# Opening of a Fourier filter and SoLU kernel: x transposed as interleaved pairs of columns and loaded in halves of 64 rows, raw weights loaded early, output weights converted in steps 0 and 1

## The chip, the cores and the metric

The kernel runs on one NeuronCore of a Trainium2 chip. A core has five engines that run their own instruction streams and meet at semaphores: TensorE (PE, whose weight loads the profile lists apart as PEld), VectorE (DVE), ScalarE (ACT), GpSimd (POOL) and SyncE (SP), and 16 DMA engines behind queues that SP, ACT and POOL fill. The metric is the device time of one execution in microseconds. Before the change it is 1617.99 us, the median of three runs (1617.08, 1617.99, 1620.11).

## The reference

The input x has 8 examples of 3136 rows and 256 columns. A global Fourier filter runs along the rows, and a feed-forward block with a SoLU and a layer norm follows, row by row.

```python
X = np.fft.rfft(x, axis=1)                                   # 8 x 3136 x 256
Y = X * (filt_r + 1j * filt_i)[None]
x = np.fft.irfft(Y, n=3136, axis=1).reshape(25088, 256)

h = x @ w_in                                                 # 256 -> 1024
e = np.exp(h - max(h)); solu = h * e / (sum(e) + 1e-9)
ln = (solu - mean(solu)) / sqrt(var(solu) + 1e-6) * g_ln
out = ln @ w_out                                             # 1024 -> 256
```

## The kernel before

A row number is split as 3136 = 49 x 64, and the transform is done as matrix products in two stages with 49-point and 64-point tables; in between, the data changes place between partitions. Rows n and N2-1-n of the 64 are treated together, as an upper half h = 0 and a lower half h = 1, which leaves NH = 32 places m for each of the 49 rows.

The work has two parts.

**The opening** (lines 415 to 631, first `ExitStack`) does example 0 on the chip, with nothing of it in DRAM. Its order is written out by hand (`tc.manual_schedule`), so every engine and every queue runs its instructions in the order of the code:

- SP, ACT and POOL issue the loads (526 to 555). `fetch_x` (509) brings x in eight pieces of four places for each half into `rows_x`, 128 partitions x 32 places x 256 columns; the first 48 of the 49 rows go by `fetch_x` and the last by `fetch_last_rows` (516). On SP then come the tables with the filters (`load_tables`, 462), three of four raw blocks of w_in (`begin`, 501), small tables, six pieces of example 1 (`fetch_second`, 457), and the filters go back to DRAM as `f_dram` (553). The weights are 64-bit floats that the kernel converts itself.
- The first products (`first_rows`, 557; PE line 558) multiply a piece of `rows_x` by `wf0_t`, and ACT copies the result back over `rows_x` (565, 572).
- `convert(0)` (585) turns raw block 0 into floats: nine DVE instructions (`load_float64`, 424, lines 430 to 444).
- `idle_row` (581) gives PE products that nobody reads; they multiply the first table by the first filter. `tables_back` (473) turns the tables through PE (480) and ACT (482).
- `turn_rows` (589, DVE line 591) transposes `rows_x` in place, 32 x 32 blocks, 64 columns in each of four instructions. It walks the 32 places for each column.
- A loop over seven units (611): `start(i + 2)` issues the forward products (PE line 318, into `pb`), `multiply` does the filter (DVE lines 339 and 340, POOL 341), `idle` keeps PE running, and `inverse` makes the back products (PE line 318, into `pc`), which ACT copies into `rows_x` (356). The third table turn stands in the loop at i = 2 (613).
- `turn_rows` again; then on DVE `convert` of blocks 2, 1 and 3 and `weight_sums` (162), four sums that a seven-product scheme for 2 x 2 blocks needs.
- `back` (402) makes the final products of example 0 (PE line 408) and ACT copies them into `y` (411).

**The steps** (1012 to 1151) work on blocks of 128 rows of `y`. Step k takes block k through the products with w_in (`product`, 759, PE line 767; `keep` and `finish` bring them out on ACT and DVE), exp, normalize, a DVE transpose (`turn`, 831), a regrouping by DMA, and, nine steps later (LAG), the products with w_out (`project`, 903). Beside that, the steps carry the Fourier work of examples 1 to 7, by the list `PLAN` (37): example 1's first products (`first`, 236, PE line 243, ACT copy 245, stored by POOL in `store_first`, 249) lie in steps 0 and 1, in each step four pieces early and four in the list `late`, its spectrum units from step 4 on. They use the two PSUM buffers of `ps_t`.

The output weights are prepared in the steps too: `load_w_out` (682) is issued before step 0, `convert_w_out(k)` (688) converts one quarter in each of steps 0 to 3 (nine DVE instructions and four of line 694 that scale by `g_sb`), and `prepare_w_out` (700) makes the mean over the rows with PE (712) and ACT (714), subtracts it (717) and makes four sums (162), in steps 3 and 4. In a step they stand ahead of the `late` jobs:

```python
        if k < 4:
            convert_w_out(k)
        if k == 3:
            prepare_w_out(0)
            prepare_w_out(1)
        if k == 4:
            for n in range(2, 7):
                prepare_w_out(n)
        for job in late[k] + loads[k]:
            job()
```

Of the kernel before, what the change touches and what calls it, by code (L numbers as in the profile page):

```python
# [17 lines left out]
P = 128  # L18
# [34 lines left out]
def dft_tables():  # L53
# [39 lines left out]
    wf0 = np.zeros((NR, 4, 32))  # L93
    wi0 = np.zeros((4, 32, NR))
    wf0[:, :, :NS] = wf.reshape(NR, NS, 4).transpose(0, 2, 1)
    wi0[:, :NS] = wi.reshape(NS, 4, NR).transpose(1, 0, 2)
    return wf.reshape(NR, NK).astype(f32), wf0.reshape(NR, P).astype(f32), wq.reshape(P, 2, 64).astype(f32), \
# [4 lines left out]
def kernel(  # L102
# [80 lines left out]
    def all_filter_rows(i0, n):  # L183

        for k, filt in enumerate((filt_r, filt_i)):
            for u in range(2):
                for quarter in range(2):
                    held = min(n, (NS - u + 1) // 2 - i0)
                    yield (slice(NQ * u + 32 * quarter, NQ * u + 32 * quarter + 32), k, held,
                           filter_rows(filt, quarter, u, i0, held))  # L190
# [10 lines left out]
    class Spectrum:  # L201
# [119 lines left out]
        def forward(self, i, pss):  # L321
            t2, de = self.t2s.pop(i), self.des[i]
            for u in range(self.shape(i)[0]):
                for r in range(2):
                    block = slice(NQ * r, NQ * r + NQ)
                    self.product(i, pss[r][NQ * u:NQ * u + NQ], lambda v: de[block, v, 0, u, :],
                                 t2[block, u::2, :])
# [18 lines left out]
        def inverse(self, i, pss, out=None):  # L346
# [6 lines left out]
            self.gs[i] = self.buffer(i, "g", [P, 4, C]) if out is None else out  # L353
            for u in range(self.shape(i)[0]):
                w = self.shape(i)[1]
                nc.scalar.copy(out=self.gs[i][:, u:2 * w:2, :], in_=pss[u][:, 0:w, :])
# [45 lines left out]
    def back(e, ch, cb, evac):  # L402
# [4 lines left out]
        for i in range(NCH):  # L407
            nc.tensor.matmul(out=psv[:, i:2 * NCH - i:2 * NCH - 1 - 2 * i, :],
                             lhsT=t4s[e, ch][:, i, cb * P:cb * P + P], rhs=wi_t, start=True, stop=True)
# [4 lines left out]

    with ExitStack() as st:
        fpool = pool("fp", 1, stack=st)
        pools = {name: pool(name + "0", bufs, stack=st)
                 for name, bufs in (("r", 1), ("p", 2))}
        rows_x = pools["r"].tile([P, NH, C], FP32, name="x_0", tag="r")
        pool("gap", 1, stack=st).tile([P, 5 * 4 * C], FP32, name="gap", tag="gap")  # L420
# [41 lines left out]
        def load_tables(i0, n, dma):  # L462
            de = fpool.tile([P, n, 2, 2, NQ], FP32, name=f"de_{i0}", tag=f"de{i0}")
            dma(out=de[:, :, 0].rearrange("p i u q -> p i (u q)"), in_=there_dram[:, i0:i0 + n, :])
            f = fpool.tile([P, n, 2, C], FP32, name=f"f_{i0}", tag=f"f{i0}")
            for place, k, held, rows in all_filter_rows(i0, n):
                dma(out=f[place, 0:held, k, :], in_=rows)
            for i in range(n):
                tables[i0 + i], filters[i0 + i] = (de, i), (f, i)
# [39 lines left out]
        def fetch_x(h, n0, n, r0, rows, dma):  # L509

            first, step = (n0, C) if h == 0 else (N2 - 1 - n0, -C)
            dma(out=rows_x[N1 * h + r0:N1 * h + r0 + rows, n0:n0 + n],
# [3 lines left out]
        def fetch_last_rows(h, odd, dma):  # L516

            row, first = N1 * h + N1 - 1, odd if h == 0 else N2 - NH + 1 - odd
            places = slice(odd, NH, 2) if h == 0 else slice(NH - 2 + odd, None, -2)
            dma(out=rows_x[row:row + 1, places],  # L520
                in_=bass.AP(tensor=x.tensor, offset=x[0].offset + ((N1 - 1) * N2 + first) * C,
                            ap=[[N2 * C, 1], [2 * C, NH // 2], [1, C]]))

        st.enter_context(tc.manual_schedule())
        wf0_t = fpool.tile([NR, P], FP32, name="wf0_t", tag="wf0")
# [3 lines left out]

        fetch_x(0, 0, NCH, 0, N1 - 1, nc.sync.dma_start)  # L530
        fetch_x(1, 0, NCH, 0, N1 - 1, nc.scalar.dma_start)
        for odd in range(2):
            for h in range(2):
                fetch_last_rows(h, odd, (nc.sync, nc.scalar)[h].dma_start)
        for i in range(1, pieces):
            fetch_x(0, NCH * i, NCH, 0, N1 - 1, nc.sync.dma_start)
            fetch_x(1, NCH * i, NCH, 0, N1 - 1, nc.gpsimd.dma_start)
            if i == 4:
                begin(0, nc.gpsimd.dma_start)
        load_tables(0, 4, nc.sync.dma_start)  # L540
        load_tables(4, 4, nc.sync.dma_start)
        load_tables(8, NP - 8, nc.sync.dma_start)
        for j in (2, 1, 3):
            begin(j, nc.sync.dma_start)
# [5 lines left out]
        fetch_second()  # L550
        for i0, n, rows in ((0, 4, P), (4, 4, P), (8, NP - 9, P), (NP - 1, 1, NQ)):
# [5 lines left out]
        def first_rows(ps, j, i, h):  # L557
            nc.tensor.matmul(out=ps[:, j], lhsT=wf0_t,
                             rhs=rows_x[0:NR, NCH * i:NCH * i + NCH, P * h:P * h + P], start=True, stop=True)

        for i in range(pieces - 2):
            ps = ps_h.tile([P, 2, 512], FP32, name=f"pa_0_{i}", tag="h")
            for h in range(KD):
                first_rows(ps, h, i, h)
            nc.scalar.copy(
                out=rows_x[:, NCH * i:NCH * i + NCH, :].rearrange("p m (h c) -> p h m c", h=KD),
                in_=ps.rearrange("p h (m c) -> p h m c", m=NCH))
        for h in range(KD):
            ps = ps_h.tile([P, 2, 512], FP32, name=f"pa_0_last_{h}", tag="h")
            for j in range(2):  # L570
                first_rows(ps, j, pieces - 2 + j, h)
            nc.scalar.copy(
                out=rows_x[:, NH - 2 * NCH:NH, P * h:P * h + P],
                in_=ps.rearrange("p j (m c) -> p (j m) c", m=NCH))
# [14 lines left out]
        def turn_rows(first, size=64):  # L589
            part = rows_x[:, :, first:first + size].rearrange("p m c -> p c m")  # L590
            nc.vector.transpose(out=part, in_=part)

        convert(0)
        idle_row(3, "idle")
        tables_back(0, 4)
        idle_row(3, "idles")
        tables_back(4, 4)
        for first in range(0, C, 64):
            turn_rows(first)
# [592 lines left out]
```

## Time and profile before

| what | value |
|---|---|
| median of three runs | 1617.99 us |
| the profiled execution: own time, span of its instructions | 1616.61 us, 1614.8 us |
| busy share of the span: PE, DVE, POOL, ACT | 96%, 79%, 70%, 57% |
| mean granted PE clock | 0.985 |
| first product on x, first forward product | 8.3 us, 41.1 us |
| second row of transposes, last back product of the opening | 68.4 us, 94.0 us |
| mean of the output weights on PE, first product with w_out | 140.7 us, 192.8 us |

The profile is of one execution. Times are from the start of its span. A row of a group has busy time and the mean of one instruction in ns, then the idle time of its engine just before, and who ended it. A row of the timeline has start, duration, engine, line, and in brackets the idle time before it and who ended it. [...] "PEclk" is the clock that was granted to PE, as a share of full speed.

### The profile page before, as it was taken

What the parts mean: (1) busy time and instruction counts of PE and PEld (TensorE: products, weight loads), DVE (VectorE), ACT (ScalarE), POOL (GpSimd) and SP (SyncE); (2) the same over time, 40 slices, a digit from 0 to 9 for tenths busy, and PEclk for the clock granted to TensorE, in tenths of its full rate; (3) what the DMA queues carried; (4) which work ended last, traced back from release to release, by engine and by line L of the source; (5) the groups of instructions that cost most, each with busy time, mean ns of one, the idle gap of its engine ahead of it and who ended that gap; (6) DMA issues with size and microseconds to landing.
All of it is one profiled execution on the core that took longest, in us unless ns stands there. A gap on an engine that the chain in (4) does not pass through costs nothing. (4 is left out here: it accounts for less than half of the span.)

```text
span 1614.8 us, 36632 instructions
## 1 busy us (share of the span) xinstructions
PE 1548.7 (96%) x12814; PEld 1063.0 (66%) x12814; DVE 1272.2 (79%) x2256; ACT 918.4 (57%) x1870; POOL 1136.9 (70%) x1335
## 2 busy tenths in 40 slices
PE   5895899999999999999999999999999999999997
PEld 2452466666666677666766676666676777777777
DVE  5787887898889879886899779886888777777673
ACT  2242565656555656566556656566556666666663
POOL 1441888669778877697678877788766766676765
PEclk9897999999999999999999999999999999999999
DMA  9534778786788678865787677866785454343434
GB/s 247 187 97 148 216 237 224 221 237 197 205 229 257 183 185 246 235 193 156 228 247 209 175 190 242 230 181 170 215 225 149 123 134 122 104 112 93 117 105 112
DMA packets 340920, 298.08 MB, mean 185 GB/s; under 512 B 28126, under 2 KB 310216, under 8 KB 340738
## 3 DMA queue, kind: packets, MB, share of 16 engines
q1 hardware_dynamic: 275362, 170.91, 40.0%
q0 software_dynamic: 30912, 91.49, 18.9%
q10 hardware_dynamic: 34464, 33.33, 6.9%
q8 instruction: 104, 1.70, 0.5%
q14 instruction: 78, 0.64, 0.1%
HBM read 118.02 MB, written 74.84 MB: 119 GB/s over the span
## 5 line engine op out<-in xcount | busy, mean ns | idle before, releaser
L903 PEld LDWEIGHTS o<-w_out_sb,solu_t 128*128 128x128 f32 x3136 | 381.7, 192 | 48.7 <-issue 43.5
L767 PE MATMUL m<-w_in_sb,s 128*128 128x512 f32 x784 | 399.3, 610 | 9.6 <-ACT h L777 4.2
L903 PE MATMUL o<-w_out_sb,solu_t 128*128 128x128 f32 x3136 | 401.2, 276 | 2.8 <-DVE ot L923 2.7
L903 PEld LDWEIGHTS o<-w_out_sb,u 128*128 128x128 f32 x2352 | 307.7, 192 | 138.4 <-issue 105.9
L767 PE MATMUL m<-w_in_sb,y 128*128 128x512 f32 x588 | 308.5, 608 | 9.3 <-DVE nmax L791 7.9
L903 PE MATMUL o<-w_out_sb,u 128*128 128x128 f32 x2352 | 310.9, 276 | 2.6 <-POOL u L746 2.1
L813 DVE SCALAR_TENSOR_TENSOR h<-e,h 128x1024 f32<-128x1024 f32 x196 | 296.2, 1511 | 0.0
L777 ACT COPY h<-m 128x512 f32<-128x512 f32 x294 | 173.3, 589 | 207.2 <-PE m L767 185.1
L919 ACT ACTIVATE ot<-o,rs_t 128x128 f32<-128x128 f32 x392 | 143.6, 368 | 246.8 <-PE o L903 244.4
L791 DVE CUSTOM_DVE_ANT_0 h<-m,h 128x512 f32<-128x512 f32 x196 | 134.2, 685 | 175.5 <-ACT h L777 101.7
L746 POOL TENSOR_TENSOR u<-solu_t 128x512 f32<-128x512 f32 x98 | 136.3, 1391 | 192.3 <-DMA solu_t<-turn 131.8
L821 ACT ACTIVATE h<-h,nmu 128x1024 f32<-128x1024 f32 x196 | 225.1, 1148 | 60.2 <-DVE turn L831 60.1
L831 DVE STREAM_TRANSPOSE turn<-h 128x1024 f32<-128x1024 f32 x196 | 243.1, 1240 | 3.5 <-DVE ot L923 0.3
L801 ACT ACTIVATE e<-h,nmax 128x1024 f32<-128x1024 f32 x196 | 225.4, 1150 | 7.7 <-DVE h L813 6.3
L746 POOL TENSOR_TENSOR u<-solu_t,u 128x512 f32<-128x512 f32 x98 | 135.8, 1385 | 96.7 <-PE o L903 95.0
L767 PEld LDWEIGHTS m<-w_in_sb,s 128*128 128x128 f32 x784 | 128.2, 191 | 96.3 <-issue 74.9
L923 DVE SCALAR_TENSOR_TENSOR ot<-o,rs_t,ot 128x128 f32<-128x128 f32 x299 | 103.7, 347 | 100.6 <-ACT ot L919 59.1
L746 POOL TENSOR_TENSOR u<-u,solu_t 128x512 f32<-128x512 f32 x98 | 159.7, 1630 | 15.2 <-PE o L903 8.5
L767 PEld LDWEIGHTS m<-w_in_sb,y 128*128 128x128 f32 x588 | 96.6, 191 | 104.1 <-issue 45.3
L746 POOL TENSOR_TENSOR solu_t<-solu_t,solu_t 128x512 f32<-128x512 f32 x98 | 150.9, 1540 | 0.9
L746 POOL TENSOR_TENSOR s<-y 128x128 f32<-128x128 f32 x196 | 99.9, 510 | 30.2 <-ACT y L411 29.7
L385 PEld LDWEIGHTS py<-wb_t,t 50*64 50x64 f32 x3584 | 57.8, 134 | 43.3 <-issue 19.4
(126 smaller groups left out, 1972.6 us busy)
## 6 DMA issues: line engine op xcount, KB each, us to landing
solu_t<-turn SPq DMA_DIRECT2D x780, 128.0 KB
out_dram<-ot SPq DMA_DIRECT2D x196, 128.0 KB
t<-d POOLq DMA_DIRECT2D x112, 200.0 KB, 6.8
d<-x POOLq DMA_DIRECT2D x100, 200.0 KB, 5.2
f<-f_dram POOLq DMA_DIRECT2D x39, 512.0 KB, 7.4
t<-d ACTq DMA_DIRECT2D x37, 512.0 KB
d<-g POOLq DMA_DIRECT2D x36, 512.0 KB, 5.0
x<-in_x_dram SPq DMA_DIRECT2D x112, 98.0 KB
```

The source lines that it names most:

```text
L385: nc.tensor.matmul(out=views[g][64 * h:64 * h + 64, cb, i, :], lhsT=t4[rows, i, c0:c0 + 64], rhs=wb_t[rows, 0:N1], start=True, stop=True)
L746: nc.gpsimd.tensor_tensor(out=out, in0=in0, in1=in1, op=op)
L767: nc.tensor.matmul(out=ms[j, bank], lhsT=lhsT, rhs=w_in_sb[:, w, :], start=m in (1, 2, 7), stop=True, skip_group_check=True)
L777: nc.scalar.copy(out=h_half(k, i), in_=ms[j, 0])
L791: nc.vector.tensor_tensor_reduce(out=h_half(k, i), in0=ms[j, bank], in1=h_half(*kept), scale=1.0, scalar=sofar, op0=ALU.add, op1=ALU.min, ...
L801: nc.scalar.activation(out=e, in_=hs[k], func=AFT.Exp, bias=nmaxs.pop(k)[:, 1:2], scale=-1.0, accum_out=esums[g][:, i:i + 1])
L813: nc.vector.scalar_tensor_tensor(out=solu, in0=e, scalar=SHRINK, in1=solu, op0=ALU.mult, op1=ALU.mult, accum_out=nmu)
L821: nc.scalar.activation(out=solu, in_=solu, func=AFT.Square, bias=nmu, scale=-float(DFF), accum_out=variances[g][:, i:i + 1])
L831: nc.vector.transpose(out=turns[g][:, :, i, :], in_=solus[k].rearrange("p (f j) -> p f j", j=32))
L903: nc.tensor.matmul(out=pos[p, bank], lhsT=lhs[:, f, :], rhs=w[:, f, :], start=f == 0 and (m in (1, 2, 7) or alone), stop=True, skip_group_ ...
L919: nc.scalar.activation(out=out_half(p, *to)[0], in_=pos[p, 0], func=AFT.Copy, scale=rs)
L923: nc.vector.scalar_tensor_tensor(out=ot, in0=pos[p, bank], scalar=rs, in1=out_half(p, *kept)[0], op0=ALU.mult, op1=ALU.add)
```

## The change

In the opening:

- x is loaded in 64 rows for each half instead of 49, the last row with the others; what lies beyond the 49 rows meets zeros in `wf0_t`, which now has 128 rows. Of the sixteen loads one is on ACT, eight on SP, seven on POOL.
- The raw blocks of w_in all go out on POOL, between the x pieces, in the order 0, 2, 1, 3. Blocks 0, 2 and 1 are converted before the first transposes, block 3 after the second.
- SP sends all tables and then all filters (`load_filters`, new), and the rows of the filters in another order, so that consecutive transfers go to partitions 0, 64, 32 and 96.
- Fourteen warm-up products stand ahead of the first products on PE. All three table turns stand before the forward products, with idle products between them.
- A first product covers two places and all 256 columns, and ACT writes its result as interleaved pairs: `pairs_x` is the same memory as `rows_x`, with the two columns of a pair of places next to each other. The transposes then walk 16 pairs for each column (`"p a c t -> p c a t"`). Forward products, back products and the copies of `inverse` take every second word.
- The product tiles of the opening have three buffers instead of two, and a placeholder tile of 20 KB a partition (`gap`) goes.
- The raw output weights have a buffer that exists from the start (`turn0`) and are loaded in the opening, behind `fetch_second` and ahead of the stores of the filters. That buffer later takes every second `turn` tile.

In the steps: two quarters of the output weights are converted in step 0 and two in step 1, and their scaling is on ACT. The mean is made in step 2, and the subtraction and sums are done in step 3.

The diff, cut to its core:

```diff
-    wf0 = np.zeros((NR, 4, 32))
+    wf0 = np.zeros((2, 64, 4, 32))
-    wf0[:, :, :NS] = wf.reshape(NR, NS, 4).transpose(0, 2, 1)
+    wf0[:, :N1, :, :NS] = wf.transpose(0, 1, 3, 2)
...
-            for u in range(2):
-                for quarter in range(2):
+            for quarter in range(2):
+                for u in range(2):
...
                     self.product(i, pss[r][NQ * u:NQ * u + NQ], lambda v: de[block, v, 0, u, :],
-                                 t2[block, u::2, :])
+                                 t2[block, u::2, :] if len(t2.shape) == 3 else t2[block, :, :, u])
...
             for u in range(self.shape(i)[0]):
-                w = self.shape(i)[1]
-                nc.scalar.copy(out=self.gs[i][:, u:2 * w:2, :], in_=pss[u][:, 0:w, :])
+                nc.scalar.copy(out=self.gs[i][:, u:2 * w:2, :] if out is None else out[:, 0:w, :, u],
+                               in_=pss[u][:, 0:w, :])
...
-                             lhsT=t4s[e, ch][:, i, cb * P:cb * P + P], rhs=wi_t, start=True, stop=True)
+                             lhsT=t4s[e, ch][:, i // 2, cb * P:cb * P + P, i % 2], rhs=wi_t,
+                             start=True, stop=True)
...
-                 for name, bufs in (("r", 1), ("p", 2))}
+                 for name, bufs in (("r", 1), ("p", 3))}
         rows_x = pools["r"].tile([P, NH, C], FP32, name="x_0", tag="r")
-        pool("gap", 1, stack=st).tile([P, 5 * 4 * C], FP32, name="gap", tag="gap")
+        pairs_x = rows_x.rearrange("p m c -> p (m c)").rearrange("p (a c t) -> p a c t", c=C, t=2)
...
+        for i in range(pieces):
+            fetch_x(0, NCH * i, NCH, 0, 64, nc.sync.dma_start)
+            fetch_x(1, NCH * i, NCH, 0, 64, nc.gpsimd.dma_start if i else nc.scalar.dma_start)
+            if i % 2:
+                begin((0, 2, 1, 3)[i // 2], nc.gpsimd.dma_start)
+        for load in (load_tables, load_filters):
+            for i0, n in ((0, 4), (4, 4), (8, NP - 8)):
+                load(i0, n, nc.sync.dma_start)
...
         fetch_second()
+        for n in range(4):
+            load_w_out(n, nc.sync.dma_start)
...
+        for j in range(14):
+            nc.tensor.matmul(out=ps_t.tile([P, P], FP32, name=f"warm_{j}", tag="t"), lhsT=one, rhs=one,
+                             start=True, stop=True)
+        for i in range(pieces):
             ps = ps_h.tile([P, 2, 512], FP32, name=f"pa_0_{i}", tag="h")
             for j in range(2):
+                nc.tensor.matmul(out=ps[:, j], lhsT=wf0_t,
+                                 rhs=rows_x[:, NCH * i + 2 * j:NCH * i + 2 * j + 2, :],
+                                 start=True, stop=True)
+            nc.scalar.copy(out=pairs_x[:, 2 * i:2 * i + 2].rearrange("p a c t -> p a t c"),
+                           in_=ps.rearrange("p a (t c) -> p a t c", t=2))
...
+        def turn_rows():
+            for first in range(0, C, 64):
+                part = pairs_x[:, :, first:first + 64].rearrange("p a c t -> p c a t")
+                nc.vector.transpose(out=part, in_=part)
+
+        for j in (0, 2, 1):
+            convert(j)
         idle_row(3, "idle")
-        tables_back(0, 4)
-        idle_row(3, "idles")
-        tables_back(4, 4)
-        for first in range(0, C, 64):
-            turn_rows(first)
+        for i0, n in ((0, 4), (4, 4), (8, NP - 8)):
+            tables_back(i0, n)
+            idle_row(2, f"idle_{i0}")
+        turn_rows()
...
         for i in range(units):
-            if i == 2:
-                tables_back(8, NP - 8)
...
-        for j in (2, 1, 3):
-            convert(j)
+        turn_rows()
+        convert(3)
         weight_sums(w_in_sb)
...
         for f in range(KF // 2):
             fg = KF // 2 * h + f
-            nc.vector.tensor_scalar(out=w_out_sb[:, i, f], in0=w_out_sb[:, i, f],
-                                    scalar1=g_sb[:, fg:fg + 1], scalar2=-1.0 / SHRINK,
-                                    op0=ALU.mult, op1=ALU.mult)
+            nc.scalar.activation(out=w_out_sb[:, i, f], in_=w_out_sb[:, i, f], func=AFT.Copy,
+                                 scale=g_sb[:, fg:fg + 1])
...
             nc.vector.memset(mean["ones"][:, 0:P], 1.0)
+            nc.vector.tensor_scalar(out=g_sb, in0=g_sb, scalar1=-1.0 / SHRINK, scalar2=None, op0=ALU.mult)
...
-            turns[g] = wk2.tile([P, DFF // 32, 4, 32], FP32, name=f"turn_{g}", tag="turn")
+            turns[g] = turn_pools[1 - g % 2].tile([P, DFF // 32, 4, 32], FP32, name=f"turn_{g}", tag="turn")
...
-        if k < 4:
-            convert_w_out(k)
-        if k == 3:
-            prepare_w_out(0)
-            prepare_w_out(1)
-        if k == 4:
+        if k == 0:
+            prepare_w_out(0)
+        if k < 2:
+            for n in range(2 * k, 2 * k + 2):
+                convert_w_out(n)
+        if k == 2:
+            prepare_w_out(1)
+        if k == 3:
             for n in range(2, 7):
                 prepare_w_out(n)
```

## The prediction

> **What bounds the kernel now.** I read the page first, then the PE's waits, then the opening instruction by instruction.
>
> ```profile
> span 1614.8 us, 36632 instructions
> ...
> PE 1548.7 (96%) x12814; PEld 1063.0 (66%) x12814; DVE 1272.2 (79%) x2256; ACT 918.4 (57%) x1870; POOL 1136.9 (70%) x1335
> ...
> PE   5895899999999999999999999999999999999997
> ```
>
> The PE is full from the sixth slice on (one slice is 40 us). Only the first 165 us have holes, so whatever the opening gains or loses reaches the end nearly one for one. The steps that follow never wait for a time of day. The timeline of the opening, with the idle time before an instruction in brackets:
>
> ```profile
> 24.60 16.38 DVE L591 STREAM_TRANSPOSE x<-x 128x2048 f32<-128x2048 f32 x4 [7.17 <-DMA f<-in_filt_r_dram]
> ...
> 41.12 4.75 PE L318 MATMUL pb<-x,de 64*64 64x256 f32 x48 [8.95 <-DVE x L591]
> ...
> 68.44 16.40 DVE L591 STREAM_TRANSPOSE x<-x 128x2048 f32<-128x2048 f32 x4 [4.49 <-ACT x L356]
> ...
> 76.76 17.25 PE L408 MATMUL py<-wi_t,x 128*128 128x98 f32 x128 [3.50 <-issue]
> ```
>
> Two rows of four transposes, 16.4 us each, stand on the path: x transform, row one, seven units of spectrum work, row two, back products (L408). The PE's waits after 100 us:
>
> ```profile
> PE m L767 <- DVE nmax L791: 9.0, 3, 3.9
> PE ps_mean L712 <- DVE ones L706: 7.8, 1, 7.8
> PE m L767 <- DVE w_in_sb L162: 3.2, 1, 3.2
> PE m L767 <- ACT h L777: 1.8, 2, 1.0
> ```
>
> All but the last are DVE late with weight conversions. So DVE sets the start of full speed, from 84.8 us (end of row two) to 158.1 us (end of the output weights).
>
> **The transposes.** The nearest rows:
>
> ```profile
> L591 DVE STREAM_TRANSPOSE x<-x 128x2048 f32<-128x2048 f32 x8 | 32.8, 4238 | 11.7 <-DMA f<-in_filt_r_dram 7.2 <-ACT x L356 4.5
> ...
> L831 DVE STREAM_TRANSPOSE turn<-h 128x1024 f32<-128x1024 f32 x196 | 243.1, 1240 | 3.5 <-DVE ot L923 0.3
> ```
>
> L591 jumps 1 KB at every element and takes 2.0 ns an element; L831 reads in order and writes runs of 32 and takes 1.2. The changed pattern jumps after every second element. Bounds for one transpose: 2.4 us (L831's rate) and 4.1 us (no gain). I take 2.4, because the cost should belong to a lone word: 0.43 us is the time of L430, which touches every second word of raw, and of L434 on adjacent words. A row becomes 9.6 us, 6.8 less.
>
> [...]
>
> **Loads.** Ahead of the first filters (f_0) stand now: x 16 x 256 KB = 4.19 MB (3.2 before), four raw weights 2.10 MB (one, 0.52, before), the tables 0.85 MB, f_0 itself 1.05 MB, small tables 0.13: 8.3 MB instead of about 5.2. From 4 to 14 us the queues moved 274 GB/s, POOL's 1.73 MB against SP's 0.92, and from 16 to 34 us, SP alone, 244. So POOL's weights go ahead of SP's filters. x and raw: 6.4 MB / 274 = 23.4 us from 2 us, x complete near 25; the remaining 1.9 MB at 244: 7.8 us. **f_0 lands near 33 us**, about 22 before by the same sum. Bounds: 31 to 36.
>
> [...]
>
> **The PE up to the forward products.** Fourteen warm-up products cover the wait for x; 16 products of 0.86 us then follow x as it lands, to about 26 us, and the last eviction (1.0 us, L565) ends at 27. Row one of DVE would end at 36.6, converts 0, 2 and 1 (4.65 us each, nine rows L430 to L444) hidden in the wait for x. But in the PE's queue, ahead of the forward products, stand three idle products that read f_0, then three table turns (13 products) with two idles after each. The idles take 0.90 us (12 records in 5.42 us), the turns 0.26: 9 x 0.90 + 13 x 0.26 = 11.5 us from 33 us. The PE has stood 7 us by then. Before, it stood from 32.2 and its granted clock fell to 0.50 by 36, and it was full again 4 us after 41.1; so 4 us at half speed add 2. Forward products start at 33.2 + 13.5 = **46.7**, against 41.1: the filters and not the transposes decide, and the faster row one is hidden.
>
> From first forward product to row two took 27.3 us. Off: the cold start (2.1 us to DVE's first multiply, now 1.2) and the table turn inside the loop (units are 2.95 us apart, one was 5.3): 3.2 less. The third product buffer saves DVE 4.1 us of waits for pc, but the cycle goes pc, ACT, idle, pc on the PE, so I take 0 (at most 2.4, if POOL's 2.55 us a unit decided). Row two starts at **70.8** (was 68.4) and ends at 80.4 (was 84.8). Back products need two of its transposes: 75.6, met by the six idles (70.0 + 5.4), so the PE comes warm; 16 x 0.90 us (0.49 copy + 0.41 wait each when warm) end at **90.0** (was 94.0).
>
> **Strided operands.** Forward products, L408's weights and ACT's copies touch every second word. No row shows this on PE or ACT. I take 0, as L430 against L434; the other end is the transposes' 2.0 / 1.2 = 1.65 times: L408 is bound by weight loads (PEld 17.1 us beside PE 17.2), so +9.3 us; forward products +2, copies +2. A gain is excluded: all these were contiguous.
>
> **Steps 0 to 5.** Converts 2 and 1 leave the tail: convert 3 and the sums (4.65 + 2.6) end at 87.6, was 103.1, so the 3.2 us wait at 102.5 goes. Two output quarters per step now, scaled by ACT: 4 x 0.37 us (L919, nearest) instead of 0.87 on DVE. This adds a wait. ACT is in order, and behind its scaling stand the evictions of the late x products (L243), which have two banks; so PE's third such product waits for the second conversion.
> - Step 0: 90.0 + 5.4 (products 1, 2, four early ones) + 1.8 = 97.2. DVE converts 92.8 to 102.2, ACT scales to 103.7, evicts to 104.3; two late products at half clock: 107.7 (109.5 before).
> - Step 1: + 6.1 = 113.8; DVE converts 114.7 to 124.0, ACT to 126.1, late products to 129.5 (119.2 before; here it is 10 late).
> - Step 2: four products and the mean (32 x 0.11): 136.9. The mean stood at 146.1.
> - Step 3: finishes, turn, normalize to 142.6, then subtract and sums 6.2: 148.8. Step 4's finish 149.6, its last products 150.5 (150.8 before).
> - Step 5: DVE owes 3.6 of step 4, then its finish: the product that started at 158.8 starts at 154.1.
>
> **Sum:** 4.7 us earlier. Against the profiled run (1616.6, span 1614.8) this is 1611.9; against the median 1618.0, which I predict for, **1613.3**. The raw output weights now load after x's second example, long before 92 us; the turn buffers keep their number.
>
> **Rivals.**
> 1. *The filters are not late* (0.20). The swapped order of the filter rows spreads consecutive transfers; were f_0 there when x is done (it needs 350 GB/s, seen at 34 to 38 us on the raw weights, 375), the transposes would decide: forward at 36.6, 10 us sooner, 1603. Against it: 244 to 274 in all of x and filters.
> 2. *Slower: strided weights in L408* (0.14). Each load costs up to 1.65 times; from 1.33 times (4.7 / 14.4) on all is lost; at 1.65 the time is 1622.6. For it: L591; against: L430.
> 3. *The transposes do not get faster* (0.08). Row one stays hidden (27 + 16.4 = 43.4 < 46.7). Row two: back products' second half at 70.8 + 16.4, ends 94.4, so 1617.7.
> 4. *Given back* (0.10): late stores of the x products (ten us late in step 1) hold up the spectrum loads of steps 4 to 8, or POOL, 98% full at 240 to 260 us, is the bound: 1616 to 1618.
>
> Forecast 0.48. Some 0.2% (3.2 us) is what a measurement can tell from no change. Faster: 0.40 of the forecast, rival 1 and a trace: 0.61. Same: rest of the forecast, rivals 3 and 4 mostly: 0.24. Slower: rival 2 and a little of rival 4: 0.15. The range reaches to rival 1's 1602 and part of the way to rival 2: 1602 to 1619.5.
>
> **What would show it.** Transposes of 2.2 to 2.5 us; a PE hole of some 7 us before the first idle, released by the filters, and forward products near 47; row two near 71; L408 at 0.11 us a weight load; L162 long before the products that need it; in steps 0 and 1 L243 waiting for ACT, and ACT for DVE, 5 and 10 us. Wrong, if the first idle doesn't wait, if L408's loads grow, or if DVE never leaves ACT waiting in step 1.

## The result, and the profile after

The changed kernel takes **1609.9 us** (median of five executions, 1607.3 to 1612.0) against 1618.0 in the same comparison (1617.1 to 1624.3): ratio 0.9939, 95% interval 0.9916 to 0.9961. Two more comparisons gave 0.9969 (0.9955 to 0.9982) and 0.9962 (0.9943 to 0.9981), with 12 executions of the changed kernel each: 5.4 and 5.8 us between the medians, where 4.7 were forecast. The first comparison's 8.1 us rests on five executions; the three intervals overlap. The profiled execution took 1609.97 us with a span of 1608.2 (before: 1616.61 and 1614.8).

The page of the changed kernel, its span, the busy times, and the PE's row of 40 slices:

```profile
span 1608.2 us, 36683 instructions
...
PE 1555.3 (97%) x12848; PEld 1066.7 (66%) x12848; DVE 1258.9 (78%) x2241; ACT 924.7 (58%) x1886; POOL 1141.3 (71%) x1338
...
PE   7976999999999999999999999999999999999997
```

DVE lost 13 us of work. The third slice (80 to 120 us) fell from 9 to 7: there is a new hole. The fourth is 6, where it was 5. First the timeline of the opening (start, duration, instruction, idle time before it and what ended that; x16 stands for sixteen equal records in a row, and PE has two records for each product, 32 for the sixteen of L568):

```profile
21.37 9.89 PE L568 MATMUL pa<-x,wf_t 128*128 128x512 f32 x16 [3.48 <-issue]
...
32.39 8.89 DVE L590 STREAM_TRANSPOSE x<-x 128x2048 f32<-128x2048 f32 x4 [3.30 <-ACT x L571]
34.02 4.41 PE L576 MATMUL idle<-f,de 128*128 128x512 f32 x6 [2.75 <-DMA f<-in_filt_r_dram]
...
46.41 3.06 PE L318 MATMUL pb<-x,de 64*64 64x256 f32 x48
...
70.80 8.89 DVE L590 STREAM_TRANSPOSE x<-x 128x2048 f32<-128x2048 f32 x4 [7.10 <-ACT x L357]
75.44 15.26 PE L410 MATMUL py<-wi_t,x 128*128 128x98 f32 x128
```

A row of four transposes takes 8.89 us instead of 16.4. But row one ends at 41.3 and the forward products start 5 us behind that: the idles of L576 waited for the filters (2.75 us, third row), and the table turns and idles behind them ran in order. The second half of the opening is the forecast to within 1 us. Next, steps 0 and 1, first by the PE's waits from 85 to 170 us, then ACT's scaling (L682) and the late products (L243) in the timeline:

```profile
PE pa L243 <- ACT y L245: 16.2, 2, 10.3
PE m L755 <- DVE nmax L779: 3.4, 1, 3.4
...
98.70 1.28 ACT L682 ACTIVATE w_out_sb<-w_out_sb,g_sb 128x128 f32<-128x128 f32 x4 [1.29 <-DVE w_out_sb L458]
103.42 1.27 ACT L682 ACTIVATE w_out_sb<-w_out_sb,g_sb 128x128 f32<-128x128 f32 x4 [3.44 <-DVE w_out_sb L458]
104.60 1.04 ACT L245 COPY y<-pa 100x512 f32<-100x512 f32 x2
...
105.21 3.73 PE L243 MATMUL pa<-y,wf_t 98*100 98x512 f32 x4 [5.84 <-ACT y L245]
...
127.12 3.73 PE L243 MATMUL pa<-x,wf_t 98*100 98x512 f32 x4 [10.34 <-ACT y L245]
```

Read the middle three rows from the end: ACT evicts the late products only at 104.60, because its queue holds the scaling of 103.42, which waited 3.44 us for DVE's conversion. The wait is PE's, the cause sits two engines away. The 16.2 us replace the 20 us of waits for DVE that the kernel before had.

### The profile page after: what moved, and what is told of

Its sections match the earlier page's. It is cut to its first block, busy times and chain, and to the rows that moved or that the text cites. A ratio compares the mean times of both kernels' runs of the same rounds, so it can differ in the third digit from the quotient of the medians.

```text
span 1608.2 us, 36683 instructions
## 1 busy us (share of the span) xinstructions
PE 1555.3 (97%) x12848; PEld 1066.7 (66%) x12848; DVE 1258.9 (78%) x2241; ACT 924.7 (58%) x1886; POOL 1141.3 (71%) x1338
## 5 line engine op out<-in xcount | busy, mean ns | idle before, releaser
L801 DVE SCALAR_TENSOR_TENSOR h<-e,h 128x1024 f32<-128x1024 f32 x196 | 307.8, 1570 | 0.0
L907 ACT ACTIVATE ot<-o,rs_t 128x128 f32<-128x128 f32 x392 | 143.2, 367 | 245.7 <-PE o L891 244.1
L819 DVE STREAM_TRANSPOSE turn<-h 128x1024 f32<-128x1024 f32 x196 | 243.1, 1240 | 3.1
L734 POOL TENSOR_TENSOR u<-solu_t,u 128x512 f32<-128x512 f32 x98 | 136.0, 1388 | 93.8 <-PE o L891 93.5
L755 PEld LDWEIGHTS m<-w_in_sb,s 128*128 128x128 f32 x784 | 129.0, 192 | 93.5 <-issue 73.1
L734 POOL TENSOR_TENSOR solu_t<-solu_t,solu_t 128x512 f32<-128x512 f32 x98 | 156.1, 1593 | 0.9
L734 POOL TENSOR_TENSOR s<-y 128x128 f32<-128x128 f32 x196 | 96.2, 491 | 26.5 <-ACT y L414 26.0
```

The lines of the kernel that those rows point to most:

```text
L734: nc.gpsimd.tensor_tensor(out=out, in0=in0, in1=in1, op=op)
L755: nc.tensor.matmul(out=ms[j, bank], lhsT=lhsT, rhs=w_in_sb[:, w, :], start=m in (1, 2, 7), stop=True, skip_group_check=True)
L801: nc.vector.scalar_tensor_tensor(out=solu, in0=e, scalar=SHRINK, in1=solu, op0=ALU.mult, op1=ALU.mult, accum_out=nmu)
L819: nc.vector.transpose(out=turns[g][:, :, i, :], in_=solus[k].rearrange("p (f j) -> p f j", j=32))
L907: nc.scalar.activation(out=out_half(p, *to)[0], in_=pos[p, 0], func=AFT.Copy, scale=rs)
```

## The experiments

The table has the profiles' marks in us: start of the forward products (L318), end of the back products (L410), end of the sums of the input weights (L162), start of the mean's product (ps_mean), then the 14th and the last turn transpose (L819, before L831); last the median time and the interval of the ratio to the kernel before. The medians come from five comparisons, in which the kernel before lay between 1617.3 and 1618.5.

| kernel | forward | back ends | sums | mean | turn 14 | last turn | median | ratio |
|---|---|---|---|---|---|---|---|---|
| before | 41.1 | 94.0 | 103.1 | 140.7 | 249.4 | 1583.6 | 1618.0 | 1 |
| before_again | 41.8 | 94.9 | 104.0 | 141.7 | 250.5 | 1582.5 | | |
| after | 46.4 | 90.7 | 86.9 | 135.5 | 246.2 | 1578.5 | 1609.9 | 0.9916 to 0.9961 |
| after_again | 45.1 | 89.4 | 85.6 | 135.3 | 247.2 | 1578.4 | | |
| after_third | 47.3 | 91.6 | 87.8 | 137.1 | 249.7 | 1585.9 | 1611.8 | 0.9955 to 0.9982 |
| after_fourth | 45.7 | 90.0 | 86.2 | 135.4 | 245.7 | 1578.8 | 1612.7 | 0.9943 to 0.9981 |
| early_idle | 39.5 | 83.8 | 80.0 | 129.0 | 240.3 | 1574.2 | 1605.8 | 0.9901 to 0.9939 |
| scale_last | 46.2 | 90.5 | 86.7 | 127.3 | 240.2 | 1570.5 | 1603.6 | 0.9896 to 0.9930 |
| both | 41.5 | 85.7 | 82.0 | 120.5 | 231.9 | 1568.9 | 1596.2 | 0.9855 to 0.9895 |
| quarters_late | 45.6 | 89.8 | 86.1 | 140.5 | 250.1 | 1584.3 | 1612.9 | 0.9964 to 0.9990 |
| no_pairs | 45.4 | 92.3 | 91.4 | 137.7 | 248.2 | 1579.9 | 1615.0 | 0.9968 to 0.9997 |
| raws_late | 40.5 | 84.7 | 93.8 | 137.2 | 248.5 | 1580.2 | 1612.4 | 0.9955 to 0.9980 |
| both_raws_late | 35.2 | 79.4 | 88.5 | 120.6 | 233.2 | 1564.3 | 1598.9 | 0.9858 to 0.9912 |
| both_spread | 39.4 | 83.7 | 79.9 | 128.2 | 236.6 | 1567.2 | 1601.7 | 0.9880 to 0.9935 |

The theory is the prediction's: two waits on the path, for the filters near 34 us and for ACT in steps 0 and 1, limit a gain that comes from DVE's relief. The rivals are that other parts carry the gain, or that something in the later steps does.

### What repeats: both kernels again

The first two profiles seemed to say that the opening's lead was lost at 246 us and a larger one appeared between 440 and 506 us. That could be the change or the single execution.

> The kernel before, unchanged, for a second profile. What is open: between the two first profiles the lead of the changed kernel was 3.3 us at the 14th turn (246 us), about 0 from the 15th to the 37th (263 to 440 us), and 7.3 us at the 45th (506 us). Theory A (chance of one execution: transfers that land a little sooner or later): the second profile does not pass the marks at the same times as the first; differences of 1 to 6 us against the first profile come and go at other turns. Theory B (the schedule is that rigid): it passes every turn within 0.5 us of the first profile, and the loss at 246 us and the gain at 440 to 506 us belong to the change.

> The changed kernel, unchanged, for a second profile. Theory A (chance of one execution): the lead over the kernel before at the 14th turn is again about 3 us, but the loss at 246 us or the gain between 440 and 506 us is not there, or is somewhere else. Theory B: 0.0 to +1.1 us at turns 15 to 37 and some -7 us from turn 45 on, again.

> The changed kernel unchanged, for more times and a third profile. The second profiles put the two kernels' spans 4.7 us apart (1612.9 and 1608.1), the medians of the first comparison 8.1. Theory A (what the opening saves, 3 to 4 us at the turns 15 to 29, is all; the rest of the 8.1 is the spread of single executions): the third profile passes turns 0 to 13 within 0.5 us of the second, and the median of the new executions lies 4 to 6 us under the kernel before's. Theory B (something in the later steps gains too): again 7 to 10 us between the medians, with the ends of the profiles 3 to 5 us further apart than turn 29.

> The changed kernel unchanged, as the measure for the two beside it on the same chip. If what the third comparison gave is right (1611.8 against 1617.25), the median is 1610 to 1613 again, 4 to 7 us under the kernel before's; if the first (8.1 us apart), 1608 to 1610.

Theory A of the first two holds. The loss at 246 us isn't in after_again (turns 15 to 21 are 3.0 to 3.7 us ahead of before_again), and of the gain from turn 37 to 45, 5.0 us are between the two profiles of the kernel before. After_third passed turn 14 2.5 us later than after_again and turn 45 10.7 us later (515.2 against 504.5): single executions drift apart by that much with nothing changed. On average over the four profiles of the changed kernel and the two of the one before, the lead is 2.7 us at turn 4 (166.7 against 169.4), 2.8 at turn 14 and 2.7 at the last turn: as far as six executions can say, what the opening gives reaches the end. In between it is not constant (-1.4 to 1.0 at turns 15 to 38, 2.0 to 5.0 from turn 45 on), by less than single executions drift. The medians, over more executions, say 5.4 and 5.8; after_fourth's 1612.7 fell in the first band of its expectation. Why the profiles show only half of that is not settled: the two profiled executions of the kernel before (1616.6 and 1614.7) are below its medians.

### The wait for the filters: early_idle

```diff
         def idle(out):
-            nc.tensor.matmul(out=out, lhsT=..., rhs=filters[0][0][:, 0], ...)
+            nc.tensor.matmul(out=..., lhsT=..., rhs=tables[0][0][:, 0:4, 0], ...)
```

> The idle products of the opening read a table that lands with x (de_0) in place of the filters f_0; their output goes nowhere, so nothing that is computed changes. Theory (the prediction's: the filters decide when the forward products start, because the idles ahead of them wait for f_0): the first idle starts right behind the x products, at 31 to 32 us instead of 34.0; the forward products then wait for row one of the transposes (ends 41.3) or for the idles, whichever is later: 41.5 to 43.5 us instead of 46.4; row two starts 3 to 5 us sooner (66 to 68 instead of 70.8), and if the opening's lead reaches the end, the time is 3 to 5 us less than the changed kernel's, 1605 to 1607. Rival 1 (the PE's cold clock takes it back: idles run at half speed): forward at 45 to 46, 1609. Rival 2 (the opening's lead is lost in steps 0 and 1, where ACT's block sets the pace from DVE's conversions): row two 3 to 5 us sooner but the turn of step 13 and the end as before, 1610.

The timeline of early_idle:

```profile
28.82 2.74 PE L576 MATMUL idle<-de 128*128 128x512 f32 x6
...
30.14 8.89 DVE L590 STREAM_TRANSPOSE x<-x 128x2048 f32<-128x2048 f32 x4 [1.39 <-DMA f<-in_filt_r_dram]
...
39.54 3.08 PE L318 MATMUL pb<-x,de 64*64 64x256 f32 x48
```

What a bracket names is inferred: row one reads no filter, and follows ACT's last eviction (ends 30.10). The six idle records take 2.74 us instead of 4.41 (the PE didn't stand before them), and the forward products start right behind the last idles, 0.5 us after row one (ends 39.0). The back products end 6.9 us sooner, 2 us more than expected. The expectation took row one's end from the changed kernel's first profile (41.3), where x was late; here row one started at 30.14 instead of 32.39, as in the other profiles of the changed kernel (30.2 to 30.7). The median is 6.0 us under the 1611.8 of after_third, which is from another comparison (the kernel before: 1617.7 here, 1617.3 there). Theory confirmed; both rivals fall.

### The wait for ACT: scale_last

```diff
         for job in late[k] + loads[k]:
             job()
+        if k < 2:
+            for n in range(2 * k, 2 * k + 2):
+                scale_w_out(n)
```

Here `scale_w_out` is the loop of four ACT instructions that `convert_w_out` ended with.

> In steps 0 and 1 the scaling of the output weights on ACT is issued behind the step's late evictions instead of ahead of them; all that is computed is the same. Theory (ACT, in order, holds the late x products): the PE's two waits for ACT's evictions (5.8 and 10.3 us) go; the late products of step 0 start near 99.5 instead of 105.2, those of step 1 near 117 instead of 127.1; then DVE with its four conversions (9.4 us a pair) sets the pace again, and the mean's product starts 5 to 9 us sooner (127 to 130 instead of 135.5), step 4's last product 3 to 8 us sooner (143 to 148 instead of 150.8); 1602 to 1607 if the lead reaches the end. Rival (DVE sets the pace anyway, and the waits only move to another place): the PE waits as long for DVE, step 4's last product at 150 to 151, 1610.

Its PE's waits from 85 to 170 us:

```profile
PE m L758 <- ACT h L768: 10.7, 4, 7.5
PE m L758 <- DVE nmax L782: 3.4, 1, 3.4
PE pa L243 <- ACT y L245: 2.2, 1, 2.2
```

The 16.2 us fall to 2.2, but 10.7 (2.3 before) are now for ACT's h (L768), which in turn stands behind the second scaling:

```profile
121.95 1.28 ACT L685 ACTIVATE w_out_sb<-w_out_sb,g_sb 128x128 f32<-128x128 f32 x4 [3.96 <-DVE w_out_sb L458]
```

Still the mean's product starts 8.2 us sooner, the 14th turn 6 us and the last 8 us; the median is 8.2 us under 1611.8. Theory confirmed, though 8.4 of the 14.0 us come back as another wait, as the rival has it. The rest is not all waiting. Between the last back product and the mean's product, the PE's idle time falls from 16.3 to 9.7 us and its busy time from 28.5 to 27.1, for the same work: in the changed kernel its granted clock there is 0.77, and the time of the products grows behind the waits. Of its late products, the four records behind the wait of 5.84 us took 3.73 us (granted clock 0.51 from 105.2 to 109.0 us), and four such records at 111.4 us took 1.94 (1.00 from 109 to 117); here the four behind the wait of 2.24 us took 2.77.

### Both edits

> The two edits together: the idles of the opening read a table that lands with x, and the scaling on ACT is issued behind the late evictions. Alone they ended 4.3 and 8.0 us (spans) before the changed kernel. Theory (two waits in a row on the path, the one before 50 us and the other from 100 to 135 us): the leads add up, the last start of step 0's turn 14 us sooner than in the changed kernel, span 1596 to 1598, time 1597 to 1600. Rival (both are paid out of the same slack: a sooner start only lengthens the next wait for DVE or, around 200 to 215 us, for POOL and the transfers): no better than the better one alone, 1601 to 1604.

Median 1596.2, 15.6 us under the changed kernel (alone 6.0 and 8.2) and ratio 0.9875 to the one before. The mean's product starts at 120.5: 15.0 us sooner than in the changed kernel, 6.5 + 8.2 = 14.7 alone. The leads add up in the sum, though not part by part: x came late in this execution (row one at 32.05), so the back products end 5.0 us sooner and not 6.9, and behind them the PE idles 9.7 us as in scale_last but is busy for 25.1 us instead of 27.1. This is the fastest kernel of the study. Its profiled execution was one of the two longest of five (1600.3), which fits a last turn that is only 9.6 us ahead.

### The output weights in steps 0 and 1: quarters_late

```diff
-            nc.vector.tensor_scalar(out=g_sb, in0=g_sb, scalar1=-1.0 / SHRINK, scalar2=None, op0=ALU.mult)
...
         if k == 0:
+            nc.vector.tensor_scalar(out=g_sb, in0=g_sb, scalar1=-1.0 / SHRINK, scalar2=None, op0=ALU.mult)
+        if k < 4:
+            convert_w_out(k)
+        if k == 3:
             prepare_w_out(0)
-        if k < 2:
-            for n in range(2 * k, 2 * k + 2):
-                convert_w_out(n)
-        if k == 2:
             prepare_w_out(1)
-        if k == 3:
+        if k == 4:
             for n in range(2, 7):
```

> Of the change, the output weights' place alone is undone: one quarter converted in each of the steps 0 to 3, the mean in step 3, subtraction and sums in step 4, as before; ACT still scales, ahead of the late evictions. Theory (the prediction: conversions in steps 0 and 1 hold up the late products there and give it back in step 5): undone, the mean's product starts near 140 us instead of 135.5 and the products of step 5 wait again for DVE, 3 to 6 us later, 1611 to 1616. Rival (DVE was relieved enough by the two opening conversions, 9.3 us, and by the scaling that ACT took over, 14 us, so that one quarter a step fits beside the step's own work, and each late product waits 1 to 2 us instead of 5.8 and 10.3): the PE's waits from 85 to 165 us fall from some 25 to under 15 us, and the kernel is faster than the changed one, 1600 to 1606.

Its PE's waits from 85 to 165 us:

```profile
PE m L754 <- ACT h L764: 7.4, 2, 6.4
PE ps_mean L699 <- DVE ones L693: 6.9, 1, 6.9
PE pa L243 <- ACT y L245: 6.2, 2, 5.6
PE m L754 <- DVE nmax L778: 3.8, 1, 3.8
```

They sum to 24.3 us against 22.4 in the changed kernel: other waits, nearly the same sum. The mean starts at 140.5, as the theory said, and the median is 1.1 us above that of after_third on the same chip, which these intervals can't tell from nothing. The rival falls. As it was made, this part of the change brings 1 us by the medians; the two intervals leave room for nothing and for some 4 us (an estimate from them).

### The pairs: no_pairs

```diff
-                part = pairs_x[:, :, first:first + 64].rearrange("p a c t -> p c a t")
+                part = pairs_x[:, :, first:first + 64].rearrange("p a c t -> p c t a")
```

> Of the change, the order in which the transposes walk is undone: the two elements of a pair are no longer taken one after the other, so that every element is again 512 words from the next; the rows inside each block then come out in another order, so the values are not the reference's, the work is the same. Each transpose takes 4.1 us instead of 2.22. Theory (the filters hide row one, row two is on the path, the prediction's third rival): row one ends at 48.8 and the forward products start 2.5 us later, near 49; row two ends 8 to 10 us later (88 to 90); the back products wait for its second half only, and end 4 to 7 us later; then 1614 to 1617 in all. Rival 1 (DVE's tail sets the pace behind it, all of row two's lateness arrives): +10 us, 1619 to 1621. Rival 2 (steps 0 to 3 have room to spare and take it in): within 2 us of the changed kernel.

```profile
30.82 14.39 DVE L590 STREAM_TRANSPOSE x<-x 128x2048 f32<-128x2048 f32 x4 [2.12 <-DMA f<-in_filt_i_dram]
...
45.36 3.05 PE L318 MATMUL pb<-x,de 64*64 64x256 f32 x48 [1.13 <-DVE x L590]
```

These are row one and the forward products in its timeline. A transpose takes 3.6 us, not 4.1. Row one costs the forward products 1.13 us of waiting and no more: the filters had hidden most of it. In this execution the idles ran without a slow stretch (2.81 us for the first six records, 4.41 in the changed kernel); with one, the wait would have been shorter still. Row two ends 14.5 instead of 8.9 us after its start, and the back products 46.9 us after the first forward product instead of 44.3. So the pairs bring 2.6 us by the trace and 3.2 by the medians (1615.0 against 1611.8), out of 5.4. That fits the theory (the prediction's third rival, +4.4), a little smaller, but the intervals of the two kernels overlap, so the medians alone don't show it.

### The early raw weights: raws_late

```diff
-            if i % 2:
-                begin((0, 2, 1, 3)[i // 2], nc.gpsimd.dma_start)
+            if i == 4:
+                begin(0, nc.gpsimd.dma_start)
...
+        for j in (2, 1, 3):
+            begin(j, nc.sync.dma_start)
...
-        for j in (0, 2, 1):
-            convert(j)
+        convert(0)
...
         turn_rows()
-        convert(3)
+        for j in (2, 1, 3):
+            convert(j)
```

> Of the change, the early raw weights alone are undone: one raw weight (0.52 MB) loads with x, the other three behind the filters, and two of the conversions go back behind row two of the transposes (9.3 us of DVE). Theory (the early weights cost the filters about 6 us, which the idles pass on to the forward products, and save DVE's tail 9.3 us, which does not stand on the path at first, for the products of step 0 need the sums at about 90 us): first idle at 27 to 29 us instead of 34, forward products at 39 to 41 instead of 46.4, row two at 63 to 66; then convert 2, 1, 3 and the sums end at 88 to 92 and the first products that need them wait 1 to 4 us; DVE reaches the output weights' conversions no sooner than now, so ACT's scaling and the late products of steps 0 and 1 stand where they stand: 1609 to 1614 in all, no measurable difference. Rival 1 (DVE's tail has room): the 6 us reach the end as in the kernel with early idles, 1604 to 1607. Rival 2 (DVE's 9.3 us push the blocks of ACT in steps 0 and 1 later by all of it): 1615 to 1619.

```profile
27.99 4.27 PE L578 MATMUL idle<-f,de 128*128 128x512 f32 x6 [3.54 <-DMA f<-in_filt_r_dram]
...
40.47 3.08 PE L318 MATMUL pb<-x,de 64*64 64x256 f32 x48
...
93.22 2.93 PE L757 MATMUL m<-w_in_sb,s 128*128 128x512 f32 x4 [3.23 <-DVE w_in_sb L162]
...
105.29 3.74 PE L243 MATMUL pa<-y,wf_t 98*100 98x512 f32 x4 [6.71 <-ACT y L245]
```

In its timeline the filters land 6 us sooner, the forward products start 5.9 us sooner, and step 0's late products start at 105.29 (105.21 in the changed kernel). DVE's rows show where the head start ends, first those of the changed kernel, then that of raws_late (L444 is the first instruction of the first output quarter):

```profile
92.59 0.69 DVE L779 CUSTOM_DVE_ANT_0 h<-m,h 128x512 f32<-128x512 f32 x1 [5.68 <-PE m L755]
...
93.36 0.48 DVE L444 TENSOR_SCALAR raw_out<-raw_out 128x512 int32<-128x512 int32 x1
```

```profile
93.79 0.42 DVE L444 TENSOR_SCALAR raw_out<-raw_out 128x512 int32<-128x512 int32 x1
```

In the changed kernel DVE is done with its sums at 86.9, and then stands 5.68 us for step 0's first product, which the later forward products make late; in raws_late the products are early and DVE still converts. The output quarters begin at the same time, and so does all that waits for them. Median 1612.4 against 1612.7: the theory's no difference, with DVE's idle time as the place where the 9.3 us saved went.

### The same with both waits gone: both_raws_late

> The kernel with early idles and late scaling, with the raw weights put back behind the filters as in raws_late. There, with the changed kernel's idles and scaling, nothing was gained or lost (1612.4 against 1612.7): the forward products came 5.9 us sooner and the late products of step 0 at the same time, 105.3, since two more conversions (9.3 us) stood ahead of them on DVE. Theory (DVE's chain of transposes, conversions and output quarters is what sets steps 0 and 1, so what the early weights do is take 9.3 us off it): x complete 3 to 4 us sooner than in the kernel with both edits, forward products at 36 to 38 instead of 39.5 to 41.5, but weight sums at 88 to 91 instead of some 80, the PE's waits for DVE's sums and ACT's h longer by 4 to 6 us: 1599 to 1603 against 1596. Rival 1 (DVE has slack now, x is what counts): 1592 to 1594. Rival 2 (cancels again): 1595 to 1598.

The forward products start 6.3 us sooner than in the kernel with both edits (35.2), the sums end 6.5 us later (88.5), and the mean's product starts at 120.6 against 120.5. By these two profiles it cancels again (rival 2). But x came some 2 us late in the profile with both edits (row one at 32.05, in most others at 30.0 to 30.8), and the PE's waits from 85 to 170 us are 21.2 us here and 17.5 there, 3.2 of them for DVE's sums, which is nearly what the theory says. The medians (1598.9 against 1596.2, with overlapping intervals and on different chips) don't decide between the two; only rival 1 falls. So without the two waits the early weights bring nothing or some 3 us; which, stays open.

### One quarter a step with both edits: both_spread

Against the kernel with both edits:

```diff
-            for n in range(2 * k, 2 * k + 2):
-                convert_w_out(n)
+            convert_w_out(k)
```

This runs for k < 4, the scaling stays behind the late jobs, and the mean is made behind those of step 3.

> The kernel with early idles and late scaling, but one output quarter in each of the steps 0 to 3 (the mean behind step 3, subtraction and sums in step 4) in place of two in steps 0 and 1. In that kernel the PE waits from 85 to 165 us were 10.7 us for ACT's h, 3.4 for nmax, 2.2 for y. Theory (as in the changed kernel itself, where this made 1 us: the waits change their place and not their sum): 1595 to 1599. Rival 1 (with ACT out of the way, one conversion of 4.7 us a step fits beside the step's work): waits under 8 us in all, 1588 to 1593. Rival 2 (mean, subtraction and sums in steps 3 and 4 hold up step 4's and 5's products, which the early quarters avoid): 1599 to 1604.

Six executions from 1596.8 to 1613.5, median 1601.7; the mean's product waits 6.9 us for DVE as in quarters_late and starts 7.6 us later than with both edits alone. The PE's waits from 85 to 170 us sum to 20.1 us (17.5 with both edits), so rival 1 falls. Its interval overlaps that of both, which ran on another chip: no gain is seen, and the theory and rival 2 stay open.

## Why the prediction was right

- **The bound.** That the steps pass on what the opening gives held within the noise: 6.0, 8.2 and 15.6 us of median for 6.5, 8.2 and 15.0 us at the mean's product.
- **Transposes.** 2.22 us (8.89 for four) where 2.4 was taken; with the two words of a pair taken apart, and nothing else changed, it is 3.60 (14.39 for four, no_pairs). No row of the kernel before shows the 2.2 at the lower end of the prediction's 2.2 to 2.5.
- **Loads.** f_0 was forecast at 33 (31 to 36); the first idle started at 34.0, in six other profiles with these loads and idles at 32.4 to 34.1. The step that failed lies ahead of row one, which started at 30.2 to 32.4 in the four profiles of the changed kernel instead of behind 27. Only part of that is x: it was to be complete at 25, and its last piece landed at 25.5 to 26.8. The rest is the PE's clock, which the prediction put at full speed there: in the first profile the PE stood 3.48 us until 21.37, its granted clock was 0.50 from then to 26.5, and the first six records took 0.86 us each instead of 0.43. Without the early weights (raws_late) the last eleven of these records took 4.88 us (0.44 each) and row one started at 25.6. The prediction set POOL's weights ahead of the filters, but they stand ahead of x's second halves on the same queue too. POOL's row in the timeline:

```profile
12.40 0.65 POOL L530 DMA_DIRECT2D x<-in_x_dram  x1 [4.85 <-DMA raw<-in_moe_w_in_dram]
```

  It cost nothing, since the filters were later still; in early_idle it is part of the path. For x and the raw weights the forecast took 274 GB/s; the changed kernel moved 264 GB/s from 4 to 14 us, with the two halves and raw weights in flight together, and 280 from 14 to 28.
- **Forward products, row two, back products.** 46.7, 70.8 and 90.0 were forecast; 45.1 to 47.3, 69.5 to 71.7, and 89.4 to 91.6 came. That the first came so close is in part luck: the filters were 0.8 us late, and what stands between the first idle and the forward products took 12.4 us instead of 13.5. The back products, whose strided weights were priced at 0, took 0.05 us a group more: 15.26 us for 16 groups (0.95) where 0.90 was used, 0.8 us in all, 6% and not the 65% of rival 2 (no run undoes the stride alone).
- **Steps 0 and 1.** ACT's block was forecast as 5 and 10 us late; PE waited 5.84 and 10.34.
- **Steps 2 to 5.** The mean was to end at 136.9 and ended at 139.3 (3.73 us from 135.53); the subtraction and sums ended at 150.0 (148.8), step 4's last product started at 150.8 (150.5). The step that failed is step 5's: the product that started at 158.8 us in the kernel before was to start at 154.1, and started at 158.1 to 159.9 in the four profiles. Three of PE's rows of the changed kernel, then two of the kernel before:

```profile
150.79 2.04 PE L755 MATMUL m<-w_in_sb,s 128*128 128x512 f32 x2 [3.38 <-DVE nmax L779]
...
155.75 2.01 PE L318 MATMUL pb<-y 64*64 64x256 f32 x16
...
159.56 1.30 PE L755 MATMUL m<-w_in_sb,y 128*128 128x512 f32 x2
```

```profile
152.82 1.11 PE L318 MATMUL pb<-y 64*64 64x256 f32 x16
...
158.82 2.07 PE L767 MATMUL m<-w_in_sb,y 128*128 128x512 f32 x2 [3.83 <-DVE nmax L791]
```

  In this first profile the PE's granted clock behind its wait of 3.38 us was 0.50 from 150.8 to 159.6 us, and the same products (L318) took 2.01 us instead of 1.11; the prediction counted no slow stretch there. In the kernel before, the slow stretch stands behind step 5's wait (0.54 from 158.8 to 164.9 us). The changed kernel doesn't lose that time, and so is 2.7 us ahead at the fourth turn (on average over the profiles), where 4.7 were to be left.
- **Rivals.** 1 is refuted by the first idle's wait: the filters moved at 280 GB/s from 30 to 37 us, faster than the 244 of the forecast, but short of the 350 that it needs. 2 is refuted by L410, 3 is what no_pairs is, and 4 isn't seen in the times; in the turns from 15 to 38 it can't be told from the drift between executions.

So the forecast of 4.7 stands against 5.4 and 5.8 of the larger comparisons. The path and the waits are the forecast ones; that the total is so close is in part luck, since the lead at the fourth turn is 2 us smaller than forecast and the medians are further apart than the marks. Of the gain, undoing the pairs takes some 3 us (within the noise), the output weights' place 1 and the early raw weights none; the rest of the change (warm-up products, third buffer, scaling on ACT, order of the filters) wasn't undone alone. What the prediction named as costs and did not question, two waits of the change's own making, were worth 15.6 us more.

## What to carry to other kernels

When a forecast lists a new wait as a price, look at what is queued behind the waiting instruction and whether it must be there: here a filler product that read a late operand cost 6.0 us of median, and a scaling ahead of evictions in ACT's queue 8.2 us, what the PE's products took longer behind the waits among them, and each was removed by an edit of a few lines. Loading and converting earlier pays only if both the transfers that are pushed back and the engine that is relieved have room; here the forward products came 6 us sooner or later and the end stayed, since DVE's relief ended in waiting for the products. And a lead that seems to vanish and come back in one profile must be looked for in a second profile of the same kernel before it is explained.

## What the runs showed of the hardware

- Transposes of 128 x 2048 words in place: 4.1 us when every word jumps 256 words (before), 3.6 us when every word jumps 512 words and the two words of a pair are taken 16 steps apart (no_pairs), 2.22 us when they are taken one after the other (after). The 3.6 was not expected; the bytes are the same, and which of its two differences from 4.1 counts wasn't tried.
- Six idle records took 2.74 us after work (early_idle). Behind 2.8 to 4.5 us without work they took 4.16 to 5.46 us in seven profiles, but 2.81 in no_pairs behind 3.67 us: the length of a wait alone doesn't tell whether the PE comes back slow.
- Where it did, the wait cost more than its own length: in the changed kernel's first profile the granted clock was 0.50 behind waits of 3.48 and 3.38 us, for 5.1 and 8.8 us, and sixteen records of L318 in the second stretch took 2.01 us instead of 1.11.
- A group of eight weight loads and products of the back products took 0.95 us in the changed kernel, whose weights are read at every second word (15.26 us for 16), against 0.90 in the kernel before; no run changes the stride alone.
- The kernel's own time varies by up to 15 us from one execution to the next (1606.2 to 1621.7 for the changed kernel on one chip), and two profiles can part by 8 us over some 260 us of steady work without any edit (turns 14 to 45 of after_again and after_third).
